# Pooled attention and top-1 experts on one core: value products in three banks handed round one by one, indices of ranked parts on VectorE, other ranks and another order

## The chip, the cores and the metric

One core of one Trainium2 chip runs the whole program in one launch. The core has TensorE (PE: matrix products, with a weight load of its own, PEld), VectorE (DVE), ScalarE (ACT), GpSimd (POOL) and SyncE (SP), each with its own queue of instructions, and 16 DMA engines. Products are summed in eight banks of PSUM; everything else lies in SBUF or in device memory. The metric is the device time of one execution in microseconds (us), the median of several runs.

## The reference

Queries are averaged in pairs, so 576 of them look at 1152 keys in each of 8 batches and 8 heads of 64 features. The 4608 rows that come out, 512 wide, go through a layer of 8 experts, of which each row takes the one with the largest gate logit.

```python
q_pool = q.reshape(B, H, S // 2, 2, D).mean(axis=3)          # B, H, S, D = 8, 8, 1152, 64
scores = scale * np.matmul(q_pool, k.transpose(0, 1, 3, 2))
scores = scores - np.max(scores, axis=-1, keepdims=True)
attn = np.exp(scores)
attn = attn / (np.sum(attn, axis=-1, keepdims=True) + 1e-09)
x = np.matmul(attn, v)                                       # -> (4608, 512)
logits = x @ w_gate                                          # w_gate (512, 8)
expert_idx = np.argmax(logits, axis=1)
gate_w = softmax(logits)[row, expert_idx]
for e in range(8):
    xe = x[expert_idx == e]
    out[expert_idx == e] = gate_w * (np.maximum(xe @ w1[e], 0.0) @ w2[e])   # w1 (512, 1024), w2 (1024, 512)
```

## The kernel before

**Attention.** The work goes by pairs of heads, and each pair by two halves of 288 queries; there are 64 such halves, eight to a batch. A half has nine score products (L543, tile `st`, two buffers of two banks each; four matmuls apiece). DVE takes each out of PSUM into the big tile `s` and keeps a running least value (L548), a small product spreads the least over the partitions (`spread`, L566), DVE makes the bias (L572), and ACT does the exponentials in three pieces (L576). POOL then adds the nine pieces of `s` up in pairs (`fold`, L622), from which PE makes the sums (L631). Nine value products (L647) go into `pa`, one tile of two banks with one buffer: ACT copies its first bank (L652), DVE adds its second bank to that (L653), and then the tile is free for the next half. With `st`, the sums and one bank for small things all eight banks are in use. Matmuls stand in a mode of small tiles there, and the profile has two records for each of them.

**Routing.** When a batch is through, logits (L722), the best expert, and a place in that expert's list are worked out (L735 to L789). Rows go to device memory (`x_runs`), and POOL scatters token numbers into `lists` (L823).

**Experts.** Two early parts of 384 rows are taken from the first seven batches; after the last batch the experts are put in order of the rows that they have left, and `RANKS` says in which parts each of them is worked: 14 ranked parts of 160 to 384 rows. A part loads its list (`li`, L908), makes an index (L918: `ix<-li,gid`; L921: four copies `rec<-li`), gathers its rows with one indirect DMA for 32 rows (L924, four of them to a tile `xr` or `xq` of 128 rows), weighs them (L1081, L1082, DVE), turns them (L1085, DVE), splits them in a high (ACT, L1089) and a low half (DVE, L1044), and multiplies: the first products (`ph`, L1138, three for each of 32 weight tiles, 96 to a part), `hh` (ACT, L1145) and `hl` (DVE, L1147), the second products (`py`, L1167, 24 for each 128 rows, 512 columns), `y` (ACT, L1185), and a scatter to the output (POOL, L1175). For the early parts SP loads the list and DVE makes the index; for the ranked parts POOL does both, in its queue with the gathers and scatters. Weights come by SP into `raw`, and ACT (L1106) and DVE (L1044) split them.

**What sets the order.** All of it is written as steps with a key, an estimated time, and the buffers they hold. A planner (`Flow`) plays the steps through: on each engine the ready step with the least key goes next, if its buffers are free by its own reckoning. A buffer comes free after the last step that holds it and an allowance (`LATE`). The sequence that comes out is fixed in the program, engine by engine. Scatters and gathers on POOL are paced: each also waits for the last PE step that the planner put ahead of it (`in_step`). Changed costs, keys and allowances therefore give another sequence.

## Time and profile before

| | us |
|---|---|
| median of three runs | 1255.66 |
| the three runs | 1249.97, 1255.66, 1256.31 |
| the profiled execution | 1251.86 |
| its span | 1250.3 |
| PE busy in the span | 1178.0 |
| POOL, DVE, ACT busy | 874.2, 769.7, 628.7 |

The span runs from the first to the last instruction; the execution has 1.56 us around it. The attention ends at about 757 us on PE, and the last scatter is issued at 1237.75 us. The granted clock of TensorE is 0.982 of full speed over the span. A busy share says how long an engine had an instruction in work, not that the work was at its best pace: a product that waits for a buffer in the middle of a run shows as a later start of the next one.

### The profile page before, as it was taken

The numbers are of one execution on the slowest core, as the hardware profiler recorded it, in microseconds if no ns is written. First come the engines' busy times: TensorE is split into PE (matmuls) and PEld (weight loads), VectorE is DVE, ScalarE is ACT, GpSimd is POOL, SyncE is SP. The second block draws the span as 40 slices with busy tenths as digits, with TensorE's granted clock in tenths as the row PEclk, the third lists the DMA queues.
The fourth block names the chain that finished last, engine by engine and source line by source line (L and its number), as shares of the span: only waits on it lengthen the run. The fifth ranks groups of instructions, "written<-read, shape, count | busy, mean of one in ns | idle before, by whom it ended". The sixth has DMA issues, their size and how long they took to land.

```text
span 1250.3 us, 33779 instructions
## 1 busy us (share of the span) xinstructions
PE 1178.0 (94%) x14157; PEld 817.4 (65%) x14157; DVE 769.7 (62%) x2080; ACT 628.7 (50%) x768; POOL 874.2 (70%) x539
## 2 busy tenths in 40 slices
PE   6999999999999999999999998968999899999995
PEld 3555555555455555555555557858888898989994
DVE  4767777767777777767767658734444453535440
ACT  3666557666566567567565446422334241423440
POOL 1999899999799799899799253576667675620110
PEclk8999999999999999999999998988999999999998
DMA  7643342353333434423424415723434352514420
GB/s 191 158 105 95 99 121 75 102 128 78 98 96 91 123 84 107 125 66 98 134 65 108 147 37 169 216 73 110 122 119 125 112 159 82 186 42 143 135 77 20
DMA packets 76082, 138.12 MB, mean 110 GB/s; under 512 B 9859, under 2 KB 33311, under 8 KB 75920
## 3 DMA queue, kind: packets, MB, share of 16 engines
q1 hardware_dynamic: 65088, 116.18, 32.6%
q0 software_dynamic: 9744, 19.64, 5.5%
q8 instruction: 114, 1.87, 0.7%
q14 instruction: 48, 0.39, 0.1%
q10 hardware_dynamic: 1088, 0.03, 0.1%
HBM read 115.04 MB, written 21.02 MB: 109 GB/s over the span
## 4 chain that ended last, share of the span: by engine, by line
PE 67%; POOL 10%; DVE 8%; issue 8%; DMA 5%; ACT 1%; POOLq 0%; SPq 0%; DVEq 0%; ACTq 0%
PE st L543 17%; PE pa L647 16%; PE py L1167 14%; PE ph L1138 12%; POOL fold L622 7%; DVE s L548 4%; PE sums L631 2%; PE st L499 2%; DMA xq<-x_runs,ix 1%; DMA xr<-x_runs,ix 1%; PE sums L617 1%; POOL lists L823 1%; DMA raw<-in_moe_w_dram 1%; PE st L505 1%; POOL out_dram L1175 1%
## 5 line engine op out<-in xcount | busy, mean ns | idle before, releaser
L548 DVE TENSOR_SCALAR_CACHE_REDUCE s<-st 128x576 f32<-128x576 f32 x576 | 419.8, 753 | 169.7 <-PE st L543 166.4
L576 ACT ACTIVATE s<-s,bias 128x1728 f32<-128x1728 f32 x192 | 322.1, 1730 | 146.4 <-DVE bias L572 142.1
L543 PE MATMUL st<-qT,kT 64*64 64x288 f32 x4608 | 362.7, 412 | 16.3 <-DVE s L548 12.6
L647 PE MATMUL pa<-s,vn 64*64 64x288 f32 x4608 | 345.6, 404 | 1.3 <-DVE xT L653 1.3
L543 PEld LDWEIGHTS st<-qT,kT 64*64 64x64 f32 x4608 | 159.4, 133 | 152.7 <-DVE s L548 65.1
L647 PEld LDWEIGHTS pa<-s,vn 64*64 64x64 f32 x4608 | 169.4, 133 | 95.7 <-DVE xT L653 6.3
L622 POOL TENSOR_TENSOR fold<-s 128x1728 f32<-128x1728 f32 x58 | 224.2, 3872 | 9.6 <-ACT s L576 9.5
L622 POOL TENSOR_TENSOR fold<-fold,s 128x1728 f32<-128x1728 f32 x58 | 224.0, 3867 | 1.0
L1138 PE MATMUL ph<-xh,w1h 128*128 128x384 f32 (+6 forms) x512 | 159.2, 311 | 17.3 <-ACT xh L1089 8.6
L924 POOL DMA_INDIRECT xr<-x_runs,ix x104 | 112.8, 1085 | 80.7 <-PE ph L1138 20.4
L1138 PE MATMUL ph<-xl,w1h 128*128 128x384 f32 (+6 forms) x512 | 157.9, 308 | 2.1 <-DVE xl L1044 2.1
L1138 PE MATMUL ph<-xh,w1l 128*128 128x384 f32 (+6 forms) x512 | 157.5, 308 | 0.0
L1175 POOL DMA_INDIRECT out_dram<-y,rec x41 | 48.6, 1185 | 137.6 <-PE py L1167 81.6
L1167 PE MATMUL py<-w2h,hl 128*128 128x512 f32 x328 | 128.9, 393 | 6.1 <-DVE hl L1147 6.1
L1167 PE MATMUL py<-w2h,hh 128*128 128x512 f32 x328 | 128.8, 393 | 0.0
L1167 PE MATMUL py<-w2l,hh 128*128 128x512 f32 x328 | 128.5, 392 | 0.0
L1147 DVE SCALAR_TENSOR_TENSOR hl<-ph,hh 128x384 fp32r<-128x384 f32 (+5 forms) x100 | 54.5, 548 | 120.0 <-ACT hh L1145 120.0
L1145 ACT ACTIVATE hh<-ph 128x384 fp32r<-128x384 f32 (+5 forms) x100 | 48.7, 487 | 151.1 <-PE ph L1138 151.1
L1138 PEld LDWEIGHTS ph<-xh,w1h 128*128 128x128 f32 x512 | 97.8, 191 | 22.2 <-DVE hl L1147 11.8
L1138 PEld LDWEIGHTS ph<-xl,w1h 128*128 128x128 f32 x512 | 97.9, 191 | 3.5 <-DVE xl L1044 2.9
L1138 PEld LDWEIGHTS ph<-xh,w1l 128*128 128x128 f32 x512 | 97.9, 191 | 0.0
L823 POOL DMA_INDIRECT lists<-re,di x48 | 45.9, 956 | 67.7 <-PE st L543 27.3
(176 smaller groups left out, 1315.6 us busy)
## 6 DMA issues: line engine op xcount, KB each, us to landing
raw<-in_moe_w_dram SPq DMA_DIRECT2D x80, 512.0 KB
qn<-in_q_dram SPq DMA_DIRECT2D x64, 384.0 KB
kn<-in_k_dram SPq DMA_DIRECT2D x32, 576.0 KB
vn<-in_v_dram SPq DMA_DIRECT2D x32, 576.0 KB
x_runs<-row SPq DMA_DIRECT2D x24, 396.0 KB
xr<-x_runs,ix POOLq DMA_INDIRECT x104, 2.7
x_runs<-empty SPq DMA_DIRECT2D x4, 297.0 KB
lists<-re,di POOLq DMA_INDIRECT x48, 6.3
```

What stands on the lines that cost most here:

```text
L543: made = nc.tensor.matmul(pt.t[to, h, :HQ], x.kT.t[up, c * P + i * D:c * P + (i + 1) * D], x.qT.t[up, cols], start=True, stop=True, tile_p ...
L548: nc.vector.tensor_scalar(s.t[:, c], pt.t[:, :, :HQ], -SCALE, None, op0=ALU.mult, op1=ALU.min, accum_out=mx.t[:, c:c + 1],)
L576: nc.scalar.activation(s.t[:, c0:c0 + n], s.t[:, c0:c0 + n], AF.Exp, bias=bias.t, scale=-1.0)
L622: add = lambda to, a, b: nc.gpsimd.tensor_tensor(to, a, b, ALU.add)
L647: made = nc.tensor.matmul(pa.t[cs, i, :HQ], x.vn.t[up, h, c, :], s.t[up, c, h], start=c == 0, stop=c == NC - 1, tile_position=(up.start, c ...
L823: ins = nc.gpsimd.indirect_dma_start(out=lists, out_offset=bass.IndirectOffsetOnAxis(ap=di.t[:, j:j + 1], axis=0), in_=re.t[:, j, :], in_o ...
L924: return nc.gpsimd.indirect_dma_start(out=x.xr[i // NQD].t[:, i % NQD, :], out_offset=None, in_=xg, in_offset=bass.IndirectOffsetOnAxis(ap ...
L1138: made = nc.tensor.matmul(view()[:, i, :], a[:, c, fp], b[:, c, :n], start=c == 0 and k == 0, stop=c == NDC - 1 and k == 2)
L1145: a = f.add("ACT", act(nb * n) - 44, lambda fs=fs, view=view: nc.scalar.activation(hidden(m)[0][:, fs, :n], view(), AF.Relu), at - 20, don ...
L1147: d = f.add("DVE", dve(nb * n), lambda fs=fs, view=view: nc.vector.scalar_tensor_tensor(hidden(m)[1][:, fs, :n], view(), 0.0, hidden(m)[0] ...
L1167: made = nc.tensor.matmul(py.t, a[:, c, hs], b[:, c % 2, :], start=c == 0 and k == 0, stop=c == NFC - 1 and k == 2)
L1175: ins = nc.gpsimd.indirect_dma_start(out=out, out_offset=bass.IndirectOffsetOnAxis(ap=x.re.t[:up, r:r + 1], axis=0), in_=y.t[:up], in_offs ...
```

## The change

- Each half's value products go into two tiles of one bank each, `pa = [bank(o), bank(o)]`, from a pool of three banks (`BANKS` 1 to 3, in place of one bank and the pair). ACT's copy frees the one, DVE's add the other.
- The index of a ranked part (L918 and L921 before, L920 and L923 after) is made by DVE instead of POOL.
- `RANKS`: the sum of rows for each rank stays; there are 13 ranked parts instead of 14, and the largest is 416 rows. Its fourth row block has 32 rows. There are 41 row blocks and 148 gathers in either program.
- Some twenty numbers of the planner: keys, costs (`spread` 130 to 185, `best` 960 to 1100, `places` 810 to 670, list loads on POOL 1400 to 1100 and later), `AHEAD` 190 to 216 (a part's gathers by key ahead of its products), `LATE` of PE 200 to 245, and 105 less for the experts' products. `K_CHAIN` is 0 and moves nothing.

```diff
-RANKS = ((384, 288), (384, 256), (384, 224), (384, 192), (384, 160), (224, 192), (352,), (160,))
+RANKS = ((384, 288), (384, 256), (352, 256), (320, 256), (288, 256), (416,), (352,), (160,))
 S_BUFS = 2
-BANKS = 5 - S_BUFS * 2
+BANKS = 7 - S_BUFS * 2
...
-K_AV = 42
+K_AV = 51
...
-AHEAD = 190
+AHEAD = 216
...
     def values(o, f, key, x, s, ready, hp, half, xT):
-        pa = hold_of("pa", lambda h: o.ps_m.tile([P, 2, 512], F32, **h.own("pa", 1)))
+        pa = [bank(o), bank(o)]
...
-                        made = nc.tensor.matmul(pa.t[cs, i, :HQ], x.vn.t[up, h, c, :], s.t[up, c, h],
+                        made = nc.tensor.matmul(pa[i].t[cs, :HQ], x.vn.t[up, h, c, :], s.t[up, c, h],
                                          start=c == 0, stop=c == NC - 1, tile_position=(up.start, cs.start))
...
-            p = f.add("PE", 452, product, key + 20.0 * c / NC, done(p, x.v, ready[c]), [pa, x.vn, s], QUADS)
-        a = f.add("ACT", act(HQ) - 44, lambda: nc.scalar.copy(xT.t[:, hp, to], pa.t[:, 0, :HQ]), key + 20, done(p), [pa, xT])
+            p = f.add("PE", 452, product, key + 20.0 * c / NC, done(p, x.v, ready[c]), [*pa, x.vn, s], QUADS)
+        a = f.add("ACT", act(HQ) - 44, lambda: nc.scalar.copy(xT.t[:, hp, to], pa[0].t[:, :HQ]), key + 20, done(p), [pa[0], xT])
         return f.add("DVE", dve(HQ), lambda: nc.vector.tensor_tensor(
-            xT.t[:, hp, to], xT.t[:, hp, to], pa.t[:, 1, :HQ], ALU.add), key + 20, done(p, a), [pa, xT])
+            xT.t[:, hp, to], xT.t[:, hp, to], pa[1].t[:, :HQ], ALU.add), key + 20, done(p, a), [pa[1], xT])
...
-            eng = nc.vector if early else nc.gpsimd
+            eng = nc.vector
...
-        p = f.carry(at, 900 if early else 1400, load, key - LEAD, [*known, *stored], [x.re, x.li], 120, 9000 * early)
-        p = f.add("DVE" if early else "POOL", 650, index, key - LEAD, done(p), [x.li, x.ix, x.re])
+        p = f.carry(at, 900 if early else 1100, load, key - LEAD, [*known, *stored], [x.re, x.li], 120, 9000 if early else 1000)
+        p = f.add("DVE", 800, index, key - LEAD, done(p), [x.li, x.ix, x.re])
...
-                    hs = slice(r * P, (r + 1) * P)
+                    hs = slice(r * P, min((r + 1) * P, TW))
+                    n = hs.stop - hs.start
...
-                            made = nc.tensor.matmul(py.t, a[:, c, hs], b[:, c % 2, :],
+                            made = nc.tensor.matmul(py.t[:n], a[:, c, hs], b[:, c % 2, :],
```

How the sequence moves shows at three places. The first is PE's queue in the third batch, where the twentieth half's value products begin. `st` rows are score products, `pa` or `m` rows value products (their number counts tiles as they are made; `m_0`, `m_1`, `m_2` are the three banks), and the L566 row is a spread. Before:

```order
L543 MATMUL st_1_3247<-qT_0_2990,kT_0_2988 64x288 x4
L543 MATMUL st_0_3252<-qT_0_2990,kT_0_2988 64x288 x4
L647 MATMUL pa_0_3166<-s_2_2815,vn_0_2495 64x288 x4
L543 MATMUL st_1_3264<-qT_0_2990,kT_0_2988 64x288 x4
L543 MATMUL st_0_3272<-qT_0_2990,kT_0_2988 64x288 x4
L543 MATMUL st_1_3278<-qT_0_2990,kT_0_2988 64x288 x4
L543 MATMUL st_0_3285<-qT_0_2990,kT_0_2988 64x288 x4
L647 MATMUL pa_0_3291<-s_3_3044,vn_0_2495 64x288 x8
L543 MATMUL st_1_3303<-qT_0_2990,kT_0_2988 64x288 x4
L566 MATMUL st_0_3310<-ident_64,top_3308 64x64 x4
```

The same place on PE after:

```order
L544 MATMUL st_0_3263<-qT_0_2961,kT_0_2959 64x288 x4
L544 MATMUL st_1_3268<-qT_0_2961,kT_0_2959 64x288 x4
L648 MATMUL m_1_3181<-s_2_2827,vn_0_2498 64x288 x2
L648 MATMUL m_2_3184<-s_2_2827,vn_0_2498 64x288 x2
L544 MATMUL st_0_3283<-qT_0_2961,kT_0_2959 64x288 x4
L544 MATMUL st_1_3288<-qT_0_2961,kT_0_2959 64x288 x4
L544 MATMUL st_0_3297<-qT_0_2961,kT_0_2959 64x288 x4
L648 MATMUL m_0_3302<-s_3_3049,vn_0_2498 64x288 x2
L648 MATMUL m_1_3305<-s_3_3049,vn_0_2498 64x288 x2
```

Between the two halves stand three score products instead of four, and the new half takes the bank that was spare and the one that ACT's copy frees. In the whole order nine runs of exactly four score products became none, runs of three went from five to three, single ones from 170 to 213; a spread is followed at once by a score product in 16 places before and in two after.

The second place is POOL's queue at the first gathers of the first ranked part (its twelve are those with `ix_10601` before and `ix_10670` after; other numbers are later parts). Before:

```order
L918 TENSOR_SCALAR ix_10651<-li_10564,gid 128x9
L921 COPY rec_3_10653<-li_10564 32x3
L921 COPY rec_3_10653<-li_10564 32x2 x3
L924 DMA xr_10670<-x_runs,ix_10601 128x132
L918 TENSOR_SCALAR ix_10685<-li_10583,gid 128x12
L921 COPY rec_4_10687<-li_10583 32x3 x4
L924 DMA xr_10670<-x_runs,ix_10601 128x132
L918 TENSOR_SCALAR ix_10711<-li_10618,gid 128x8
L921 COPY rec_5_10713<-li_10618 32x2 x4
L924 DMA xr_10670<-x_runs,ix_10601 128x132
```

POOL's queue at that place after:

```order
L910 DMA li_10691<-lists 128x1x22
L926 DMA xr_10703<-x_runs,ix_10670 128x132
L886 TENSOR_LOAD ranked
L910 ISA
L910 DMA li_10721<-lists 128x1x16
L926 DMA xr_10703<-x_runs,ix_10670 128x132 x3
L926 DMA xq_10820<-x_runs,ix_10670 128x132 x4
L926 DMA xr_10910<-x_runs,ix_10670 128x132 x4
L1178 DMA out_dram<-y_10686,rec_0_9662 4608x512
```

No index stands between the gathers any more; the list loads and scatters of output stay on POOL. The third place is DVE's queue in the second early part's first products, around its first `hl`. Before:

```order
L1044 TENSOR_TENSOR w2l_10578<-raw_10328,w2h_10577 128x1024
L1044 TENSOR_TENSOR w2l_10598<-raw_10493,w2h_10597 128x1024
L952 TENSOR_REDUCE t_rf<-t_past 1x25
L952 TENSOR_SCALAR t_sT<-sid 1x25
L952 TENSOR_TENSOR t_sT<-t_sT,t_tu 1x25
L1044 TENSOR_TENSOR w2l_10626<-raw_10506,w2h_10625 128x1024
L1147 SCALAR_TENSOR_TENSOR hl<-ph_10608,hh 128x384
```

DVE's queue at that place after:

```order
L1046 TENSOR_TENSOR w2l_10642<-raw_10439,w2h_10641 128x1024
L920 TENSOR_SCALAR ix_10670<-li_10599,gid 128x12
L923 COPY rec_2_10672<-li_10599 32x3 x4
L1046 TENSOR_TENSOR w2l_10662<-raw_10557,w2h_10661 128x1024
L1046 TENSOR_TENSOR w2l_10694<-raw_10570,w2h_10693 128x1024
L1149 SCALAR_TENSOR_TENSOR hl<-ph_10677,hh 128x384
L920 TENSOR_SCALAR ix_10732<-li_10632,gid 128x9
L923 COPY rec_3_10734<-li_10632 32x3
L923 COPY rec_3_10734<-li_10632 32x2 x3
L920 TENSOR_SCALAR ix_10749<-li_10647,gid 128x12
L923 COPY rec_4_10751<-li_10647 32x3 x4
L1149 SCALAR_TENSOR_TENSOR hl<-ph_10710,hh 128x384
```

Before, only splits of weights and pieces of the slot table (L952) stand there. After, the first index stands ahead of the last two low halves of the second weights and of the part's first `hl`, and the next two between its first two `hl`.

## Rows read from the trace of the kernel before

**Rows 1.** The page: engines' busy time, and the chain that ended last by engine.
```profile
PE 1178.0 (94%) x14157; PEld 817.4 (65%) x14157; DVE 769.7 (62%) x2080; ACT 628.7 (50%) x768; POOL 874.2 (70%) x539
...
PE 67%; POOL 10%; DVE 8%; issue 8%; DMA 5%; ACT 1%; POOLq 0%; SPq 0%; DVEq 0%; ACTq 0%
```

**Rows 2.** Stretches (the windows view): start and end, length, then busy time of PE, PEld, DVE, ACT and POOL with instructions in brackets, the granted clock, the DMA share, GB/s. Two batches of the attention, two stretches around the first ranked part, and one late stretch of the experts.
```profile
494.10:584.80 90.70, 87.37 (x1422) 50.11 (x1418) 64.78 (x196) 53.80 (x62) 85.46 (x35) 1.00 0.38 103
584.80:677.20 92.40, 88.79 (x1450) 49.67 (x1446) 67.82 (x205) 60.03 (x67) 84.60 (x35) 1.00 0.38 100
800.00:840.00 40.00, 32.36 (x149) 27.88 (x147) 14.63 (x25) 10.72 (x18) 26.65 (x47) 0.91 0.42 129
840.00:880.00 40.00, 32.78 (x157) 29.68 (x158) 17.64 (x31) 10.31 (x18) 26.25 (x33) 0.91 0.35 102
...
1100.00:1200.00 100.00, 100.00 (x619) 91.30 (x619) 45.20 (x64) 38.99 (x61) 13.29 (x12) 1.00 0.37 117
```

**Rows 3.** The chain of work that ended last, pieces in order of time: start, length, engine, line and records.
```profile
740.12 4.37 PE pa L647 x72
...
866.48 16.36 PE py L1167 x72
882.84 6.32 PE ph L1138 x48
...
945.95 11.51 PE ph L1138 x96
...
1035.66 10.70 PE ph L1138 x60
...
1062.72 10.70 PE ph L1138 x96
...
1183.43 15.46 PE ph L1138 x96
```

**Rows 4.** Timeline of POOL, 776 to 850 us.
```profile
802.48 1.25 POOL L918 TENSOR_SCALAR ix<-li,gid 128x12 int32<-128x12 int32 x1 [2.12 <-DMA li<-lists]
...
811.08 1.16 POOL L924 DMA_INDIRECT xr<-x_runs,ix  x1 [0.45 <-POOL rec L921]
...
813.94 0.62 POOL L921 COPY rec<-li 32x3 int32<-32x3 int32 x3 [0.63 <-DMA xr<-x_runs,ix]
...
817.69 0.62 POOL L921 COPY rec<-li 32x2 int32<-32x2 int32 x3 [1.24 <-DMA xr<-x_runs,ix]
...
837.46 1.00 POOL L924 DMA_INDIRECT xr<-x_runs,ix  x1 [0.30 <-issue]
838.76 1.34 POOL L924 DMA_INDIRECT xr<-x_runs,ix  x1 [0.30 <-issue]
```

**Rows 5.** Timeline of DVE, 800 to 840 us.
```profile
823.58 0.18 DVE L1081 TENSOR_TENSOR xr<-xr,li 128x16 f32<-128x16 f32 x1 [10.11 <-DMA xr<-x_runs,ix]
...
825.15 0.52 DVE L1147 SCALAR_TENSOR_TENSOR hl<-ph,hh 128x384 fp32r<-128x384 f32 x1
...
836.21 0.17 DVE L1081 TENSOR_TENSOR xq<-xq,li 128x16 f32<-128x16 f32 x1 [8.81 <-DMA xq<-x_runs,ix]
```

**Rows 6.** Timeline of PE, 814 to 847 us: the second early part's second products, and the first ranked part's first product.
```profile
814.21 0.39 PE L1167 MATMUL py<-w2h,hh 128*128 128x512 f32 x1
...
825.72 0.79 PE L1167 MATMUL py<-w2h,hl 128*128 128x512 f32 x1 [6.10 <-DVE hl L1147]
826.31 0.63 PE L1167 MATMUL py<-w2h,hh 128*128 128x512 f32 x1
826.74 0.63 PE L1167 MATMUL py<-w2l,hh 128*128 128x512 f32 x1
...
845.26 0.69 PE L1138 MATMUL ph<-xh,w1h 128*128 128x384 f32 x1 [5.95 <-ACT xh L1089]
```

**Rows 7.** Stretches again, L1138 alone: the first products of the five ranked parts of 384 rows, each from its first to its last start; columns as in rows 2 (PE, PEld).
```profile
845.26:866.32 21.06, 19.10 (x96) 18.22 (x96) 0.87 0.41 125
911.68:929.42 17.74, 16.95 (x96) 16.48 (x95) 1.00 0.49 160
968.20:988.82 20.62, 17.27 (x96) 16.47 (x95) 1.00 0.49 152
1026.81:1046.20 19.39, 16.97 (x96) 16.49 (x95) 1.00 0.47 155
1084.17:1102.07 17.90, 17.22 (x96) 16.43 (x95) 1.00 0.53 165
```

**Rows 8.** Groups of instructions (the lines view): count, busy time and mean ns of one, then idle time before them and what ended it.
```profile
L921 POOL COPY rec<-li 32x3 int32<-32x3 int32 (+2 forms) x56 | 15.5, 277 | 18.3 <-DMA xq<-x_runs,ix 6.3 <-DMA xr<-x_runs,ix 5.1 <-DMA out_dram<-y,rec 4.5
...
L918 POOL TENSOR_SCALAR ix<-li,gid 128x12 int32<-128x12 int32 (+6 forms) x14 | 7.2, 515 | 3.3 <-DMA li<-lists 2.3
...
L921 DVE COPY rec<-li 32x3 int32<-32x3 int32 x8 | 1.3, 158 | 0.1
L918 DVE TENSOR_SCALAR ix<-li,gid 128x12 int32<-128x12 int32 x2 | 0.5, 230 | 0.0
```

**Rows 9.** Timeline of all engines, 953.2 to 954 us: a split of weights on DVE and a gather on POOL.
```profile
953.30 1.23 DVE L1044 TENSOR_TENSOR w1l<-raw,w1h 128x1024 fp32r<-128x1024 f32 x1 [0.24 <-ACT w1h L1106]
...
953.41 1.98 POOL L924 DMA_INDIRECT xq<-x_runs,ix  x1 [0.42 <-PE ph L1138]
```

**Rows 10.** The tile view of `li`: from the issue of a list load to its landing.
```profile
DMA to landing us min/median/max: 2.2/3.0/5.7
```

**Rows 11.** Timeline of the third batch, 236.9 to 241 us, PE and DVE: start, length, engine, line and operation, count, and in square brackets the idle time before it and what ended it.
```profile
237.50 1.39 PE L543 MATMUL st<-qT,kT 64*64 64x288 f32 x16
...
238.97 0.75 DVE L548 TENSOR_SCALAR_CACHE_REDUCE s<-st 128x576 f32<-128x576 f32 x1
...
239.11 1.39 PE L543 MATMUL st<-qT,kT 64*64 64x288 f32 x16 [0.21 <-DVE s L548]
...
239.65 0.45 DVE L653 TENSOR_TENSOR xT<-xT,pa 128x288 f32<-128x288 f32 x1
...
240.32 0.91 PE L647 MATMUL pa<-s,vn 64*64 64x288 f32 x12
```

**Rows 12.** Timeline of PE, 411 to 416 us, around a spread.
```profile
413.63 0.34 PE L566 MATMUL st<-ident,top 64*64 64x64 f32 x8 [0.29 <-DVE s L548]
414.48 0.72 PE L543 MATMUL st<-qT,kT 64*64 64x288 f32 x8 [0.51 <-DVE bias L572]
```

More of the change, by code (lines that the diff above doesn't have):

```diff
@@ L59 @@
 DMA = 2000
-KEEP = 20
+KEEP = 21
 LAST = 3
@@ L64 @@
 WARM = 2
-SWITCH = 150
+SWITCH = 110
 CALM, CALM_X = 700, 500
-LATE = dict(PE=200, DVE=130, ACT=130, POOL=60, SP=100, DMA=1700, DMA2=1700)
+LATE = dict(PE=245, DVE=130, ACT=130, POOL=60, SP=100, DMA=1700, DMA2=1700)
 OWN = dict(PE=0, DVE=200, ACT=220, POOL=100, SP=0, DMA=0, DMA2=0)
@@ L506, in turn @@
                                             ident[up, up], tile_position=(up.start, 0))
-            s = f.add("PE", 27 * 2 * (nk + len(qs)), turn, key, after, [pt, *([kT, kp] if ks else []), *([qT, qp] if qs else [])], ROWS)
+            s = f.add("PE", 31 * 2 * (nk + len(qs)), turn, key, after, [pt, *([kT, kp] if ks else []), *([qT, qp] if qs else [])], ROWS)
             o.turned.append(s)
@@ L789, in count @@
                 nc.vector.tensor_scalar(tok, tok, float(NQ), None, op0=ALU.add)
-        p = f.add("DVE", 960, best, at + 2, done(*weighed), [*chain, pt])
-        e = f.add("ACT", 230, lambda: nc.scalar.activation(ex.t, ex.t, AF.Exp), at + 2, done(p), [ex])
-        p = f.add("DVE", 1080, first, at + 2, done(p), [pt, ohb])
-        r = f.add("PE", 360, rank, at + 3, done(p), [pr, ohb])
-        w = f.add("DVE", 640, weight, at + 3, done(p, e), [ex, re, pt])
-        p = f.add("DVE", 810, places, at + 3, done(r, w), [pr, pt, de, di])
-        c = f.add("DVE", 400, count, at + 4, done(p), [pt, lw, ex, de])
+        gap = K_CHAIN if b is not None and b < B - 2 else 0
+        p = f.add("DVE", 1100, best, at + 2 + gap, done(*weighed), [*chain, pt])
+        e = f.add("ACT", 230, lambda: nc.scalar.activation(ex.t, ex.t, AF.Exp), at + 2 + gap, done(p), [ex])
+        p = f.add("DVE", 920, first, at + 2 + 2 * gap, done(p), [pt, ohb])
+        r = f.add("PE", 360, rank, at + 3 + 2 * gap, done(p), [pr, ohb])
+        w = f.add("DVE", 640, weight, at + 3 + 3 * gap, done(p, e), [ex, re, pt])
+        p = f.add("DVE", 670, places, at + 3 + 4 * gap, done(r, w), [pr, pt, de, di])
+        c = f.add("DVE", 400, count, at + 4 + 5 * gap, done(p), [pt, lw, ex, de])
         def put(g):
```

37 lines of the change are left out of this document (19 added, 18 removed).

## The prediction

> **What bounds the kernel now.** I read the page first. PE is busy for 1178.0 of 1250.3 us and makes up 67% of the chain that ended last; POOL and DVE follow with 10% and 8% [rows 1]. So the kernel goes at the pace of PE, and what can be won is PE work taken out, or places where PE stands or creeps. The windows show where these are. In a steady batch PE is busy for 87.37 of 90.70 us, and POOL, the next, for 85.46 [rows 2]: little is idle there, though a run of products that waits for buffers can count as busy in part. Around the first ranked part PE is busy for only 32.36 and 32.78 us of 40, and the granted clock falls to 0.91, while from 1100 to 1200 it is never idle [rows 2]. The timeline of those stretches then names the wait, and the chain gives the price of products at full pace.
>
> **Parts of the experts (term A).** A part's first products are 96 matmuls whatever its width. The chain prices 96 of them at 10.70 us for 192 columns, 11.51 for 256, 12.64 for 288 (48 in 6.32), 15.46 for 352, and 17.1 for 384 (60 in 10.70) [rows 3]. I take 10.7 for 160 and 224 as well, since the group's products of 192 columns are at what looks like a floor, 14.05 for 320 (halfway from 288 to 352), and 18.6 for 416 (1.5 past 384, by the slopes on either side, 1.4 to 1.6 for 32 columns). Before: 5 x 17.1 + 12.64 + 11.51 + 6 x 10.7 + 15.46 = 189.3. After: 2 x 17.1 + 2 x 12.64 + 4 x 11.51 + 2 x 15.46 + 14.05 + 18.6 + 10.7 = 179.8. The second products are priced by row blocks, 24 matmuls of 512 columns or 5.45 us each (72 in 16.36 [rows 3]), and both programs have 41. **A = -9.5**, between -9.2 and -9.8.
>
> **Start of the ranked parts (term B).** Here POOL decides. The first list lands, the index is made at 802.48, the first gather goes at 811.08 and the twelfth at 838.76: 28 us for twelve gathers that follow one another every 1.30 us when nothing stands between them [rows 4]. Between them stand the indices of later parts, whose copies `rec` each time wait for the gather just issued to land (at 813.94 and 817.69 [rows 4]). DVE stands for 10.11 us before it can weigh the first tile, with an `hl` queued behind; PE lacks that `hl` for 6.10 us in the middle of the second early part, and once it goes on, its products start 0.43 us apart (826.31 to 826.74) where they take 0.227 at full pace [rows 3, 5, 6]. A second wait of 8.81 us on DVE for the next tile leaves PE idle for another 5.95 [rows 5, 6]. So the second products of that part took from 814.21 to 845.26, 31.05 us for 16.36 of work, and the next first products 21.06 for 17.1 [rows 3, 6, 7]: 14.7 + 4.0 = 18.7 us lost.
>
> After the change the index is off POOL, and the queue there shows twelve gathers with one list load among them, each paced by a product of the second early part. What is new is that DVE's first index waits for the list, with two splits of second weights and the first `hl` behind it; those in turn hold back ACT and PE. An index costs DVE 0.23 + 4 x 0.158 = 0.86 us [rows 8], a split 1.23 [rows 9]. Before, POOL had the list at 802.48 [rows 4]; if DVE has it then too, the first `hl` comes after it by one index and two splits, 3.3 us, and I put the end of the first products 4.3 us later for it: **B = 4.3 - 18.7 = -14.4**. Bounds: -18.7 if the list is there before DVE comes to it, since the last `lists` scatter stands earlier in PE's order; -10 if it takes 5.7 us to land in place of the median of 3.0 [rows 10] and two more indices fall in ahead of that `hl` (4.4 us more).
>
> **Later gathers (term C).** The other four parts of 384 rows took 17.74, 20.62, 19.39 and 17.90 us, 75.65 in sum where 4 x 17.1 = 68.4 is their work [rows 7]: 7.2 us of waiting for gathered rows in the middle of the first products. POOL lost 7.2 + 15.5 us in indices and 3.3 + 18.3 in waiting for them [rows 8], 44.3 over 14 parts, and it made the gathers late by as much. Without these, and with gathers that stand earlier by key (`AHEAD` 190 to 216), they should lie a whole second product ahead: **C = -7**, between 0 and -7.2. DVE takes 13 x 0.86 = 11 us in exchange, beside a PE that is busy all the while: from 1100 to 1200 DVE has 45.20 of 100 us in work [rows 2]. The cover is gone only where the index itself has to wait for its list, which takes 2.2 to 5.7 us from issue to landing [rows 10].
>
> **Attention (term D).** A value product takes 0.485 us in a run (72 records in 4.37 [rows 3]). Where four score products stand in a row, PE goes at the pace at which DVE takes them: from 237.50 to 240.32 are 2.82 us for four, 0.88 more than 4 x 0.485 [rows 11]. They stand in a row because the next half's value products need the tile that DVE adds at 239.65 [rows 11]. After the change such runs are gone (nine to none): -7.9. A spread that a score product follows costs a wait for the bias, 0.51 us in the row shown [rows 12]; 16 such places become two. Some of these have other work that is late anyway, so I take -6 for 14 of them. Against this the new order has a third more single score products, 43 of them, which would cost 2 us at 0.05 each; that is an estimate without a row, since single ones in the trace of before don't stand out. **D = -12**, between -18 and 0; a loss is not excluded, as the keys move folds and sums too: in the new order a half's sums stand somewhat nearer to its scores, so that POOL, busy for 85.46 of 90.70 us [rows 2], has less time to fold. Ahead of the first batch and behind the last scatter I see nothing that changes.
>
> **Sum.** -9.5 - 14.4 - 7 - 12 = -42.9. From the profiled execution's 1251.86 us that gives 1209. The profiled execution is 3.8 us under the median of the three runs, 1255.66; I don't add that, since the three spread over 6.3 us. About 0.5%, 6.3 us, is what a measurement of this kernel can tell from no change.
>
> **Rivals.** *Attention gives nothing.* POOL's folds would become the last of a half. For: POOL has only 5 us of air in a batch [rows 2], and sums that stand earlier find it late. Against: the air is over three times what D asks of a batch, 1.5 us. Price: D is gone, 1251.86 - 31 = 1221.
>
> *The gathers stay late.* They are paced by products, and each needs some 2.8 us to land (the copies after the gather at 811.08 go on at 813.94 [rows 4]); if that and not the index set the pace, B and C are gone and A and D stay: 1230. Against it speak gathers every 1.30 us where no index lies between, paced in the same way.
>
> *DVE's index stops POOL.* The gather at 953.41 took 1.98 us beside a split of weights on DVE, against 1.00 alone [rows 4, 9]. If each index stopped POOL for its own length, 13 x 0.86 = 11 us would come back at worst: 1220; at the start alone, six indices, 5 us: 1214. The Trainium skill (SBUF — State Buffer, "Who interferes with whom") says that a copy or a tensor_scalar of DVE can hold the port pair that it shares with GpSimd for the whole instruction, and that the other then blocks fully. The longer gather agrees with such a rule as far as it goes, though the split is an instruction with two inputs in SBUF, which the page lists apart.
>
> *All of the waits are only moved.* Both of the first two: A alone is left, 1242.
>
> *Slower: DVE waits for lists.* Each index stands in DVE's queue ahead of `hl` and of the splits. If each found its list just issued, DVE would stand for up to 5.7 us [rows 10], 13 times, and PE behind it: 74 us, so 1283. It decides, that is, eats up the gain, from 43 / 13 = 3.3 us for each. Against it: in the new order only the first few indices stand close to their list's load; for later ones enough products stand between that, at 0.178 to 0.227 us each [rows 3], they make 4 us or more.
>
> *The change doesn't do what it says.* The names of the banks in the new order show the pairs going round, and no index on POOL, so only the size is open.
>
> **How the numbers follow.** Forecast (1209): 0.50. Attention gives nothing (1221): 0.22. Gathers late (1230): 0.14. DVE stops POOL (1214 to 1220): 0.06. Both first rivals (1242): 0.05. DVE waits for lists: 0.03. The forecast's own bounds are 1251.86 - 9.8 - 18.7 - 7.2 - 18 = 1198 and, with B at -10 and C at half, 1217. The range 1195 to 1234 leaves out the last two cases, 0.08, and the tails of the others, some 0.1. Faster by over 0.5% than the median, so under 1249.4: 0.94, all but the slower case and 0.03 of the case at 1242, whose neighbours reach that far. Within 0.5%: 0.03. Slower: 0.03.
>
> **What would show it.** Right: a batch of 90.5 to 91 us; no run of four score products, and no wait of a value product for L654's add; twelve gathers of the first ranked part within 17 us; no PE idle time over 2 us between the second early part and the end; the four parts of 256 columns at 11.5 us each. Wrong on B: PE idle in the second early part with DVE waiting for `li` or for `xr`. Wrong on C: an idle DVE before `xq` or `xr` with PE behind it. Wrong on D: batches of 92 us with waits for folds or for DVE's takes. Wrong on the whole: waits of DVE's index for `li` of several us in every part.

## The result, and the profile after

| | before | after |
|---|---|---|
| median, us | 1253.33 (4 runs) | 1223.37 (4 runs, 1221.79 to 1224.7) |
| profiled execution, us | 1251.86 | 1222.86 |
| its span, us | 1250.3 | 1221.3 |

The ratio is 0.9761, with a 95% interval from 0.9728 to 0.9794: 30 us faster. The forecast was 1209, so 14 us of the 43 are missing, and the time lies close to the first rival's 1221, though not for that rival's reason. The page of the changed kernel, its busy times and its chain by engine:

```profile
PE 1169.4 (96%) x14061; PEld 826.4 (68%) x14061; DVE 781.7 (64%) x2145; ACT 629.7 (52%) x768; POOL 854.4 (70%) x468
...
PE 78%; POOL 6%; DVE 5%; issue 4%; DMA 4%; ACT 2%; POOLq 0%; SPq 0%; DVEq 0%
```

PE's share of the chain went from 67 to 78% [rows 1]. Two batches, and the stretch from the second early part's first product to the end of the first ranked part's first products (windows view of the changed kernel, columns as in rows 2):

```profile
446.88:535.92 89.04, 87.64 (x1436) 53.88 (x1432) 66.58 (x200) 57.03 (x63) 85.21 (x35) 1.00 0.41 104
535.92:625.30 89.38, 87.97 (x1436) 53.71 (x1432) 66.58 (x200) 57.12 (x63) 85.20 (x35) 1.00 0.40 104
779.95:840.02 60.07, 52.53 (x265) 48.70 (x264) 36.19 (x87) 21.12 (x32) 34.62 (x32) 0.94 0.55 167
```

Batches take 89.0 to 89.4 us instead of 90.7 to 92.4 [rows 2], with POOL at 85.2 as before: it did not become the bound. The whole attention, from the start of its first score product to the start of its last value product, went from 737.5 (13.67 to 751.15) to 722.1 us (12.52 to 734.58). Where four score products stood in a row [rows 11], PE's timeline of the changed kernel has this:

```profile
234.24 1.39 PE L544 MATMUL st<-qT,kT 64*64 64x288 f32 x16
235.84 0.72 PE L544 MATMUL st<-qT,kT 64*64 64x288 f32 x8 [0.21 <-DVE s L549]
236.38 0.67 PE L648 MATMUL m<-s,vn 64*64 64x288 f32 x8
```

and DVE's timeline this:

```profile
236.38 0.45 DVE L654 TENSOR_TENSOR xT<-xT,m 128x288 f32<-128x288 f32 x1
```

The new half begins while the add that it used to wait for is only starting. The part around the first ranked part took 60.07 us instead of 69.92 (796.40 to 866.32 in the trace of before), 9.85 less where 14.4 were forecast. Its DVE and POOL rows:

```profile
786.84 0.23 DVE L920 TENSOR_SCALAR ix<-li,gid 128x12 int32<-128x12 int32 x1 [6.70 <-DMA li<-lists]
786.98 0.67 DVE L923 COPY rec<-li 32x3 int32<-32x3 int32 x4
787.69 2.36 DVE L1046 TENSOR_TENSOR w2l<-raw,w2h 128x1024 fp32r<-128x1024 f32 x2
789.96 0.55 DVE L1149 SCALAR_TENSOR_TENSOR hl<-ph,hh 128x384 fp32r<-128x384 f32 x1
...
791.27 0.23 DVE L920 TENSOR_SCALAR ix<-li,gid 128x12 int32<-128x12 int32 x1
791.41 0.85 DVE L923 COPY rec<-li 32x3 int32<-32x3 int32 x4
```

```profile
780.10 0.78 POOL L910 DMA_DIRECT2D li<-lists  x1 [6.03 <-DMA lists<-re,di]
...
787.90 1.96 POOL L926 DMA_INDIRECT xr<-x_runs,ix  x1 [2.07 <-DVE rec L923]
...
790.88 1.07 POOL L926 DMA_INDIRECT xr<-x_runs,ix  x1 [0.30 <-issue]
...
810.86 1.26 POOL L926 DMA_INDIRECT xr<-x_runs,ix  x1 [0.37 <-PE py L1170]
```

and PE's row behind them (its timeline, then the windows view of all engines, columns as in rows 2):

```profile
790.57 0.69 PE L1140 MATMUL ph<-xh,w1h 128*128 128x384 f32 x1 [6.22 <-DVE hl L1149]
...
790.57:793.00 2.43, 2.43 (x8) 2.43 (x9) 2.30 (x13) 0.00 (x0) 1.07 (x2) 0.50 0.88 298
```

DVE stands 6.70 us for the list, the two splits and the `hl` come behind it as the order said, and PE waits 6.22; the products right behind that wait go at a granted clock of 0.50, the lower level of 1.2 GHz. After that the second products run without a break (16.7 us instead of 31.05), and the first ranked part begins without a wait: its twelve gathers, from 787.90 to 810.86, are in time. Of the ranked parts, the first gained (18.46 us instead of 21.06 [rows 7]), but PE waits in it and in three later ones (first products alone, windows view, columns as in rows 7; widths 384, 352, 320 and 288):

```profile
821.56:840.02 18.46, 17.13 (x96) 16.66 (x95) 1.00 0.48 156
942.52:960.41 17.89, 15.86 (x96) 15.15 (x95) 1.00 0.55 167
999.67:1021.68 22.01, 16.96 (x96) 16.51 (x95) 0.84 0.40 125
1060.93:1074.72 13.79, 13.31 (x96) 12.76 (x95) 1.00 0.64 201
```

The part of 320 rows takes 22.01 us for some 14.3 of work, and the granted clock falls to 0.84 in it. Two rows of the chain say why, and that one more thing had changed:

```profile
903.43 16.70 PE py L1170 x72
...
1001.53 7.22 DMA xr<-x_runs,ix
```

The timelines of DVE and PE show the wait, and the windows view what follows it:

```profile
1008.88 0.18 DVE L1083 TENSOR_TENSOR xr<-xr,li 128x16 f32<-128x16 f32 x1 [5.78 <-DMA xr<-x_runs,ix]
1009.70 0.88 DVE L1149 SCALAR_TENSOR_TENSOR hl<-ph,hh 128x320 fp32r<-128x320 f32 x2
...
1010.24 0.63 PE L1140 MATMUL ph<-xh,w1h 128*128 128x320 f32 x1 [5.05 <-DVE hl L1149]
...
1010.24:1013.00 2.76, 2.76 (x10) 2.76 (x11) 0.34 (x1) 0.00 (x0) 0.00 (x0) 0.50 0.00 0
```

A gather takes 7.22 us from issue to landing; DVE stands 5.78 for it with two `hl` queued behind, PE waits 5.05 for the first of them, and then goes at a granted clock of 0.50 (1.2 GHz) for a while. Counted through, this gather is the 115th of the 148 and belongs to the third part further on, whose first product comes at 1091. The wait in the first ranked part is of the same kind: DVE weighs rows of the next part at 829.34, after 2.21 us for their gather, and PE lacks the `hl` behind it for 1.32. So were the waits of this stage before the change; DVE and PE in the part that began at 1026.81 [rows 7], in the trace of before:

```profile
1034.24 0.17 DVE L1081 TENSOR_TENSOR xr<-xr,li 128x16 f32<-128x16 f32 x1 [3.92 <-DMA xr<-x_runs,ix]
1035.06 1.01 DVE L1147 SCALAR_TENSOR_TENSOR hl<-ph,hh 128x384 fp32r<-128x384 f32 x2
...
1035.66 0.44 PE L1138 MATMUL ph<-xh,w1h 128*128 128x384 f32 x1 [2.42 <-DVE hl L1147]
```

And 72 second products take 16.70 us where they took 16.36 [rows 3].

### The profile page after: what moved, and what is told of

It reads as the page before. It is cut to its first block, busy times and chain, and to the rows that moved or that the text cites. A ratio compares the mean times of both kernels' runs of the same rounds, so it can differ in the third digit from the quotient of the medians.

```text
span 1221.3 us, 33596 instructions
## 1 busy us (share of the span) xinstructions
PE 1169.4 (96%) x14061; PEld 826.4 (68%) x14061; DVE 781.7 (64%) x2145; ACT 629.7 (52%) x768; POOL 854.4 (70%) x468
## 4 chain that ended last, share of the span: by engine, by line
PE 78%; POOL 6%; DVE 5%; issue 4%; DMA 4%; ACT 2%; POOLq 0%; SPq 0%; DVEq 0%
PE st L544 19%; PE m L648 18%; PE py L1170 17%; PE ph L1140 15%; POOL fold L623 5%; PE sums L632 3%; DVE s L549 2%; PE st L500 2%; PE sums L618 1%; POOL lists L825 1%; ACT s L577 1%; DMA xr<-x_runs,ix 1%; PE st L506 1%; DMA lists<-re,di 1%; DMA xq<-x_runs,ix 1%
## 5 line engine op out<-in xcount | busy, mean ns | idle before, releaser
L544 PE MATMUL st<-qT,kT 64*64 64x288 f32 x4608 | 372.3, 410 | 9.9 <-DVE s L549 6.7
L648 PE MATMUL m<-s,vn 64*64 64x288 f32 x4608 | 363.2, 405 | 0.0
L544 PEld LDWEIGHTS st<-qT,kT 64*64 64x64 f32 x4608 | 169.5, 133 | 140.0 <-DVE s L549 57.0
L648 PEld LDWEIGHTS m<-s,vn 64*64 64x64 f32 x4608 | 182.1, 133 | 84.6 <-ACT xT L653 2.6
L1140 PE MATMUL ph<-xh,w1h 128*128 128x384 f32 (+6 forms) x480 | 152.5, 318 | 17.8 <-DVE hl L1149 15.0
L1140 PE MATMUL ph<-xl,w1h 128*128 128x384 f32 (+6 forms) x480 | 151.0, 315 | 0.5 <-DVE xl L1046 0.5
L1140 PE MATMUL ph<-xh,w1l 128*128 128x384 f32 (+6 forms) x480 | 150.5, 313 | 0.0
L1170 PE MATMUL py<-w2h,hh 128*128 128x512 f32 (+1 forms) x328 | 129.6, 395 | 0.0
L1170 PE MATMUL py<-w2h,hl 128*128 128x512 f32 (+1 forms) x328 | 129.3, 394 | 0.0
L1170 PE MATMUL py<-w2l,hh 128*128 128x512 f32 (+1 forms) x328 | 128.9, 393 | 0.0
L1140 PEld LDWEIGHTS ph<-xh,w1h 128*128 128x128 f32 x480 | 92.4, 193 | 22.0 <-DVE hl L1149 17.2
L1188 ACT COPY y<-py 128x512 f32<-128x512 f32 (+3 forms) x41 | 24.0, 586 | 124.0 <-PE py L1170 114.7
```

Source lines behind the costliest of these rows:

```text
L544: made = nc.tensor.matmul(pt.t[to, h, :HQ], x.kT.t[up, c * P + i * D:c * P + (i + 1) * D], x.qT.t[up, cols], start=True, stop=True, tile_p ...
L648: made = nc.tensor.matmul(pa[i].t[cs, :HQ], x.vn.t[up, h, c, :], s.t[up, c, h], start=c == 0, stop=c == NC - 1, tile_position=(up.start, c ...
L1140: made = nc.tensor.matmul(view()[:, i, :], a[:, c, fp], b[:, c, :n], start=c == 0 and k == 0, stop=c == NDC - 1 and k == 2)
L1170: made = nc.tensor.matmul(py.t[:n], a[:, c, hs], b[:, c % 2, :], start=c == 0 and k == 0, stop=c == NFC - 1 and k == 2)
```

## The experiments

Kernels were timed in three groups, each on a chip of its own beside the kernel before. The chips differ (before: 1253.8, 1265.4 and 1257.2 us), so times are compared as ratios, and stages by the trace. "Attention" is as above; "rest" runs from the start of the last value product to the end of the last second product. On the second chip the four kernels have an attention of 728 to 730 us where the same runs of products took 722 to 724 on the others, so there the rest is read; no trace of the kernel before was kept on that chip, so what of the rest is the chip's own is not known. b_tw416 and b_ixdve have the attention of before in the same order, on two chips, at 739.4 and 739.0 us against 737.5: a difference of 2 us there says nothing.

| kernel | median, us | ratio to before | 95% | attention | rest |
|---|---|---|---|---|---|
| before (first profile) | 1253.33 | | | 737.5 | 485.7 |
| changed | 1223.37 | 0.9761 | 0.9728 to 0.9794 | 722.1 | 473.7 |
| b_banks | 1243.59 | 0.9931 | 0.9909 to 0.9952 | 731.6 | 483.6 |
| a_pair | 1255.25 | 0.9999 | 0.9974 to 1.0024 | 746.1 | 482.5 |
| b_tw416 | 1260.22 | 1.0051 | 1.0028 to 1.0073 | 739.4 | 495.3 |
| a_ranks | 1217.4 | 0.9716 | 0.9673 to 0.9758 | 721.9 | 471.2 |
| a_ixpool | 1242.83 | 0.9834 | 0.9807 to 0.9861 | 727.6 | 487.3 |
| a_g3000 | 1218.38 | 0.9637 | 0.9611 to 0.9664 | 728.2 | 463.4 |
| a_l6000 | 1225.73 | 0.9702 | 0.9673 to 0.973 | 728.5 | 469.5 |
| m_parts384 | 1230.54 | 0.9731 | 0.9701 to 0.9761 | 730.0 | 474.6 |
| b_ixdve | 1241.14 | 0.987 | 0.9827 to 0.9913 | 739.0 | 474.3 |
| m_gl | 1209.69 | 0.9619 | 0.9577 to 0.966 | 722.4 | 459.3 |
| a_kav42 | 1240.53 | 0.9854 | 0.9808 to 0.99 | 728.9 | 484.3 |
| a_h448 | 1219.15 | 0.9685 | 0.9639 to 0.9731 | 723.8 | 469.3 |

**b_banks: the three banks alone, in the kernel before.**

```diff
-BANKS = 5 - S_BUFS * 2
+BANKS = 7 - S_BUFS * 2
...
-        pa = hold_of("pa", lambda h: o.ps_m.tile([P, 2, 512], F32, **h.own("pa", 1)))
+        pa = [bank(o), bank(o)]
```

> The kernel before with the value products' halves in three banks, and nothing else of the change. In its order, runs of four score products between value products fall from 12 (with the start-up) to 1, and a spread is followed by a score product in 5 places instead of 16. Theory (the banks bring the attention's gain): the first product of the experts starts some 10 to 13 us earlier than the 757.4 us of before, the experts' stage keeps its length, and the time is about 1241. Rival (the keys and the new order bring it, the banks alone nothing): within 4 us of before, about 1250.

The time is 10 us less, but only 5.9 of it in the attention, and most batches still take 88 to 92 us. All but one of the runs of four did go, as the order said; runs of three (11 instead of 5) and of five and more (4 instead of 1, without the 12 at the start) came in their place. All runs of three and more, the 12 at the start aside, lasted 14.4 us longer in the trace than 0.485 us a product, where they had cost 12.7 before and cost 4.8 in the changed kernel. Neither theory holds as it stood.

**a_pair: the pair of banks again, in the changed kernel** (the diff above the other way round, with the changed keys).

> The changed kernel with the value products in one tile of two banks again (one spare bank, keys and the rest as changed). In its order there are 11 runs of four score products and 6 spreads followed by a score product. Theory (banks): the experts start 8 to 12 us later than the 740.8 us of the changed kernel, and the time is about 1232 to 1235. Rival (keys): at most 3 us later, under 1227.

All of the gain is gone: the attention takes 746.1 us, 24 more than the changed kernel's, twice what the theory asked, and 8.6 more than before the change. So the changed keys and costs alone are worse than nothing, the banks alone bring 5.9, and both together 15.4. The steady batches have the same order: from the first score product of the fourth batch to that of the eighth, a batch takes 91.4 us before, 92.4 in a_pair, 90.0 in b_banks and 89.1 in the changed kernel.

**a_kav42: one key back.**

```diff
-K_AV = 51
+K_AV = 42
```

> The changed kernel with the key of value products at its old 42 instead of 51. In its order there are 13 runs of three to six score products instead of 6. Theory (the banks give the freedom, the key puts the value products where they break up the runs of score products): 4 to 8 us more than the changed kernel, ratio to before 0.979 to 0.983. Rival (the banks and any key do): ratio 0.976 to 0.978.

The attention is 6.8 us longer than the changed kernel's, as expected in size, but the ratio misses the theory's range (0.985 for 0.979 to 0.983), and the theory's reason is not shown. Runs of three and more do come back, at 11.2 us instead of 4.8, but a steady batch takes 89.2 us, as with the key at 51 (89.1). The loss is in the second batch (2.6 us) and behind the first score product of the last (3.8). In the trace its last product ends 18 us later than the changed kernel's, which was not expected: the last batch's routing is no longer filled with the early part's products. From its last value product to the first product of the experts 17.8 us pass instead of 6.3, at a granted clock of 0.65 (742.25 to 760.05, windows view).

```profile
742.25:760.05 17.80, 5.48 (x47) 3.19 (x39) 15.18 (x33) 13.06 (x27) 14.29 (x12) 0.65 0.60 188
```

**b_tw416: only the distance between rows, in the kernel before.**

```diff
-    TW = max(n for ns in RANKS for n in ns)
+    TW = 416
```

> The kernel before with room for 416 columns in the tiles of tokens and hidden values (so rows of 1664 bytes instead of 1536), parts and all else as before. Theory (the distance between rows sets the rate): three row blocks of second products take 16.70 us instead of 16.36, over 41 row blocks 4.6 us more, first products of 256 and 352 columns some 1 per cent less; in sum 2 to 4 us more than before. Rival (the partial row block, or something else in the changed kernel, makes the second products slower): 16.36 stays and so does the time.

The chain has this for second products; the partial row block and the other parts are not in this kernel:

```profile
872.64 16.70 PE py L1167 x72
```

The theory holds for the rate. The time is 6 us longer instead of 2 to 4; in the trace, which is of the slowest of ten executions, the first products of three parts of 384 rows, the second early one among them, take 1.0 to 3.2 us longer too.

**a_h448: rows of 1792 bytes for the hidden values, in the changed kernel.**

```diff
-            m.h = tuple(m.w.tile([P, NFC, TW], F32R, name=a) for a in ("hh", "hl"))
+            m.h = tuple(m.w.tile([P, NFC, 448], F32R, name=a) for a in ("hh", "hl"))
```

> The changed kernel with rows of 1792 bytes (room for 448 columns) in the hidden values, 1664 in the tokens. Theory one (products whose weights come from rows that aren't a multiple of 512 bytes apart are slower): second products stay at 16.70 us for three row blocks. Theory two (a multiple of 256 bytes does): 16.36 again, 4.6 us less.

Theory two: the chain has the old rate again, and the rest is 4.4 us shorter.

```profile
906.26 16.34 PE py L1170 x72
```

**a_ranks: the parts of before, in the changed kernel.**

```diff
-RANKS = ((384, 288), (384, 256), (352, 256), (320, 256), (288, 256), (416,), (352,), (160,))
+RANKS = ((384, 288), (384, 256), (384, 224), (384, 192), (384, 160), (224, 192), (352,), (160,))
```

> The changed kernel with the parts of before (16 first products of parts instead of 15, 384 columns at most, so rows of 1536 bytes). Theory (distance between rows): second products at 16.36 us for three row blocks again, 4.6 us less in sum, against 9.5 us more for the first products by the prediction's term A: about 1228. Rival (second products at 16.70 whatever the parts): about 1233.

Both theories expected it to be slower than the changed kernel, by 5 us and by 10. It is not: 0.9716 against 0.9761, with intervals that overlap. Second products are at 16.36 for 72 and 4.6 us less in sum; first products, with one part more, take only 2.0 us more (238.2 against 236.2, the stretches from first to last start added), because the waits are smaller: 6.2 us in the later parts of 384 rows where the changed kernel has 11.2 in its three of 352, 320 and 288. In the two traces the new parts by themselves are a loss of some 2.5 us in the rest.

**m_parts384: the changed parts without the one of 416.**

```diff
-RANKS = ((384, 288), (384, 256), (352, 256), (320, 256), (288, 256), (416,), (352,), (160,))
+RANKS = ((384, 288), (384, 256), (352, 256), (320, 256), (288, 256), (224, 192), (352,), (160,))
```

> The changed kernel with its parts except for the last but two: 224 and 192 rows in place of one part of 416, so that no part is over 384 rows and rows are 1536 bytes apart. Theory (term A holds for the parts and the distance between rows costs 4.7 us): against the changed kernel second products 4.6 us less, first products 3.3 us more by 10.7 + 10.7 - 18.1, 0.8 less in the four parts of 384: 2 us less, and 5 us less than the same kernel with the parts of before, 1217.4, so 1212 to 1221. Rival (narrower first parts of an expert bring gathers and weights of the next closer together, and PE waits there): no faster than with the parts of before, 1217 or more.

The rival: 0.9731, no faster than a_ranks. Second products are at 16.36, yet the parts of 352, 320 and 288 rows take 18.83, 21.85 and 15.00 us, 13 more than without waits (15.46, 14.16 and 13.05 in m_gl below).

**a_ixpool: the index on POOL again, in the changed kernel.**

```diff
-            eng = nc.vector
+            eng = nc.vector if early else nc.gpsimd
...
-        p = f.add("DVE", 800, index, key - LEAD, done(p), [x.li, x.ix, x.re])
+        p = f.add("DVE" if early else "POOL", 800, index, key - LEAD, done(p), [x.li, x.ix, x.re])
```

> The changed kernel with the index of ranked parts on POOL again. Theory (POOL's index makes the first gathers late, as in the prediction's term B): from the first to the twelfth gather of the first ranked part 24 to 28 us instead of 23, DVE waits for rows with hl behind, PE idle 5 us or more in the second early part's second products; 6 to 10 us more, 1230 to 1233. Rival (the landing of lists and gathers sets the pace, not the engine of the index): within 3 us of 1223.

The theory, and by the trace more than its 6 to 10 us: the rest is 13.5 us longer (by the ratios it is some 9). The first ranked part's twelve gathers take 28.7 us from the first to the last issue instead of 23.0. PE's timeline has the two gaps of before [rows 6] again, somewhat wider:

```profile
817.10 0.79 PE L1170 MATMUL py<-w2h,hl 128*128 128x512 f32 x1 [8.87 <-DVE hl L1149]
...
836.84 0.69 PE L1140 MATMUL ph<-xh,w1h 128*128 128x384 f32 x1 [6.80 <-ACT xh L1091]
```

and POOL's timeline has its copies that wait for gathers:

```profile
801.79 1.13 POOL L926 DMA_INDIRECT xr<-x_runs,ix  x1 [0.28 <-POOL rec L923]
...
805.32 0.63 POOL L923 COPY rec<-li 32x3 int32<-32x3 int32 x3 [1.85 <-DMA xr<-x_runs,ix]
```

**b_ixdve: the index on DVE alone, in the kernel before** (the same lines the other way).

> The kernel before with the index of ranked parts on DVE and nothing else of the change. Theory (the index on POOL makes the first gathers late): the second early part's second products take 16.4 us instead of 31, its first products 20 to 25 instead of 17.8, since DVE stands for the first list with hl behind it; 7 to 10 us less than before, a ratio of 0.992 to 0.995. Rival (only together with the other order does it help): ratio 0.998 or more.

More than expected: a ratio of 0.987, 16 us; in the trace the rest is 11.4 us shorter. The second products of the second early part take 16.36 us, its first products 28.34, with DVE at the index for 8.99 us:

```profile
805.05 0.23 DVE L918 TENSOR_SCALAR ix<-li,gid 128x12 int32<-128x12 int32 x1 [8.99 <-DMA li<-lists]
```

The later waits fell too: parts of 384 rows at 17.61, 16.67, 18.98 and 17.23 us, 3.8 over four times 16.67, where before they were 9.0 over. One thing did not come as the prediction had it: with no index between them the twelve gathers still take 28.6 us from first to last, as before (27.7). What moved is the first of them, from 14.7 to 8.4 us after the second early part's first product.

**a_g3000: gathers are given 3 us more to land.**

```diff
-... [x.ix, x.xr[i // NQD]], 400, paced=CALM if early else CALM_X)
+... [x.ix, x.xr[i // NQD]], 400, 0 if early else 3000, paced=CALM if early else CALM_X)
```

> The changed kernel in which the planner allows 3 us more for a ranked part's gathers to land, so that the weighing of gathered rows stands later in DVE's queue, behind more of the hl. The attention's order is the same. Theory (PE's waits in the later parts, 2.1, 5.4 and 0.7 us, come from DVE standing at a weighing for rows that land in 5 to 7 us beside loads of weights, with hl behind it): these waits go, 6 to 8 us less, about 1216. Rival (the gathers are issued too late for their part, wherever DVE waits for them): the waits move to the first products of the next part, within 2 us of 1223.

In time the theory, and more than it asked: the rest is 10.3 us shorter. The same parts of 384, 352, 320 and 288 rows as in the windows of the changed kernel:

```profile
828.37:846.53 18.16, 17.18 (x96) 16.78 (x96) 1.00 0.48 156
949.04:964.40 15.36, 15.36 (x96) 15.23 (x95) 1.00 0.60 179
1003.71:1018.00 14.29, 14.29 (x96) 13.92 (x95) 1.00 0.61 204
1057.20:1070.40 13.20, 13.10 (x96) 12.74 (x95) 1.00 0.70 224
```

PE no longer waits in the last three. But the reason is not the one expected. Of 41 weighings, 33 stand behind exactly as many `hl` as in the changed kernel; of the four in front of its longest waits (829.34, 953.15, 1008.88 and 1070.10), three do, and the fourth stands behind one fewer. The row at 1008.88 of the changed kernel, on DVE here:

```profile
1006.61 0.48 DVE L1149 SCALAR_TENSOR_TENSOR hl<-ph,hh 128x320 fp32r<-128x320 f32 x1
1007.01 0.16 DVE L1083 TENSOR_TENSOR xr<-xr,li 128x16 f32<-128x16 f32 x1
...
1007.84 0.49 DVE L1149 SCALAR_TENSOR_TENSOR hl<-ph,hh 128x320 fp32r<-128x320 f32 x1
```

It has the same place, behind the part's first `hl`, and no wait. What moved is the gather: it was issued 1.9 us after the first product of the part of 320 rows (1001.53 against 999.67), and the same one, by its place among the 148, goes 3.5 us ahead of that product here (1000.2 against 1003.7). The last gathers of those four tiles go 10, 26, 27 and 31 products earlier in PE's order. So the run shows that an earlier gather takes the waits away; a later weighing was not tried.

**a_l6000: lists are given 5 us more to land.**

```diff
-..., load, key - LEAD, [*known, *stored], [x.re, x.li], 120, 9000 if early else 1000)
+..., load, key - LEAD, [*known, *stored], [x.re, x.li], 120, 9000 if early else 6000)
```

> The changed kernel in which the planner allows 5 us more for a ranked part's list to land, so that the first index stands behind both last splits of weights and three more hl of the second early part. Theory (DVE stands 6.7 us at the first index for the list, with the splits and the hl behind it): the second early part's first products take 18 to 19 us instead of 24.9; 4 to 6 us less, about 1218. Rival (the gathers come later by as much as DVE is freed): PE waits for the first ranked part's rows instead, within 2 us of 1223.

The rest is 4.2 us shorter, at the lower end of the theory. Here the waiting step did move back: the first index stands behind both splits and two `hl` (three had been expected), and DVE's waits for lists fall from 10.9 to 1.2 us.

```profile
790.92 0.56 DVE L1149 SCALAR_TENSOR_TENSOR hl<-ph,hh 128x384 fp32r<-128x384 f32 x1 [0.48 <-ACT hh L1147]
791.89 0.23 DVE L920 TENSOR_SCALAR ix<-li,gid 128x12 int32<-128x12 int32 x1 [0.41 <-DMA li<-lists]
```

The early part's first products fall from 24.90 to 18.99 us, but its second products and the next first products give back 2.35 and 1.34 (19.06 and 19.80), where the rows now come later: part of the rival.

**m_gl: these together.** The parts of m_parts384 with both allowances.

> The changed kernel with no part over 384 rows (224 and 192 in place of 416), 3 us more allowed for gathers to land and 5 us more for lists. Theory (the three causes add up: distance between rows, DVE's standing for gathers, DVE's standing for the first list): the experts' stage takes 452 to 455 us where the changed kernel took 467.5, ratio to before about 0.960. Rival (the waits of the parts with 352 to 384 rows come back, as they did with these parts and the old allowances): stage 462 or more, ratio 0.966 or more.

The rest is 459.3 us, and from the first product of the experts to the last 453.0, as the theory has it; the ratio is 0.9619, 1209.69 us, the fastest kernel here, though a_g3000 (0.9637) lies within its interval. The parts of before with both allowances were not tried, so the new parts are not shown to help here either. Behind the second early part's start PE waits for more than 1 us only once, and the four narrower parts run clean:

```profile
819.41 0.44 PE L1140 MATMUL ph<-xh,w1h 128*128 128x384 f32 x1 [4.31 <-ACT xh L1091]
```

## Why the prediction was right, and where it was wrong

The range held the time and the sign was right. Of the terms, in the profiled execution's own numbers: -29.0 us in all, of them -16.6 up to the last value product, +0.1 to the second early part, -9.85 there, -2.2 from there to the end of the last product, and -0.5 in the tail. That the time still fell into the range is in part luck: from the last value product on, -12.4 came where A, B and C had -30.9, and ahead of it more than D had, most of it by things that D had not named. Of the signs named beforehand, batches came out better (89.0 to 89.4 us for 90.5 to 91), and two failed: the twelve gathers took 23.0 us where 17 was the bound, and PE stood over 2 us twice, for 6.22 and 5.05.

**A, the parts.** The mechanism was right; the size in clean products is -8.4 (170.5 before and 162.1 after for the parts behind the first ranked one, taken from parts in which PE doesn't wait). The price of 17.1 for 384 columns came from 60 products that weren't all at full pace; 96 without a wait take 16.67. What failed is the step "both programs have 41" row blocks at 5.45 us each: the wider tiles, which I had not priced, made each row block 0.113 us dearer, +4.0 over the 35 row blocks behind that point. b_tw416 and a_h448 show that it is the distance between rows. In sum the new parts brought nothing, as a_ranks shows: the dearer row blocks took back half, and the waits of the narrower parts the rest.

**B, the start of the ranked parts.** That the index on POOL cost the stall in the second early part was right, shown both ways by b_ixdve and a_ixpool; that indices spread the twelve gathers holds in the new order (a_ixpool: 28.7 us against 23.0) and not in the old (b_ixdve: 28.6 against 27.7). The step "I put the end of the first products 4.3 us later" was too small: 7.1 (24.90 against 17.81). The list was there 6.89 us after the part's start and not, as before, 6.08, and the splits took 2.36 us behind it, as reckoned. The rest is the clock, which the step left out: 24.90 us less 16.87 of work and 6.22 of waiting leaves 1.8, for products at 0.50 of the clock behind the wait. The first ranked part's own products gained 2.6 instead of 4.0, for PE waits 1.32 us in it for an `hl` behind a weighing of the next part's rows.

**C, the later gathers.** This failed. The step "it made the gathers late by as much" put all of the 7 us down to POOL's indices. Measured against 16.67, four parts lost 9.0 us before, and after the change three parts lose 11.2, with POOL free of the index. b_ixdve shows that in the old order the index was worth 5.2 of the 9.0. In both orders PE waits for `hl`, behind a weighing at which DVE stands for a gather. The new order has its gathers too late for the place that it gives their weighings, and `AHEAD` at 216 did not mend that; a_g3000, with the gathers earlier and the weighings where they were, takes the waits away. I had written that an idle DVE before `xr` with PE behind it would show C wrong, and that is the row at 1008.88.

**D, the attention.** -15.4, and 1.2 more ahead of it, where -12 stood, inside the bounds. The step "such runs are gone: -7.9" measures -6.4 in the trace (9 runs of four, 7.7 us over 0.485 a product; one new run of five after, 1.3). The spreads gave 4.4 (16.0 to 11.6 us in all). The finer alternation cost 4.8 where I put 2: single value products with a score product behind went from 136 to 213 and their excess from 4.7 to 9.5 us. So the steps that I named come to -6.0, half of D, and that D was near is luck; the remaining 9.4 us are in work that I had not counted and that no run takes apart. And the reason given was only half of one: b_banks frees the banks and brings 5.9 us, a_pair gives the keys without the banks and loses 8.6. The bank is what allows another order; the keys are the order. What each of the other keys does was not tried.

**Rivals.** POOL did not become the bound of the attention (85.2 us busy of 89). The gathers did stay late in the later parts, as the second rival had it, but not in the first ranked one, and what made them late is their place in the order, which a_g3000 moves. DVE's index doesn't stop POOL: the gather at 790.88 took 1.07 us beside two indices, while the one at 787.90 took 1.96 beside splits of weights. By the page that I named (the Trainium skill, SBUF — State Buffer, "Who interferes with whom") an instruction of DVE with two inputs in SBUF contends with one of GpSimd that reads SBUF: the split is such a one, and the trace agrees with that part of it. The slower rival's mechanism, a DVE that waits for lists, is there twice (10.9 us in two waits for `li`), at the start, and nowhere later.

## What to carry to other kernels

Here DVE took its work in the order of its queue, so a step that stood for a transfer held up all that was queued behind it. There are two cures: issue the transfer earlier (a_g3000: 3 us more for a landing in the planner's reckoning, and no faster transfer, were worth 10 us), or put the step that waits further back (a_l6000: worth 4). When such a plan is changed, look in the trace which of the two moved. A buffer that comes free earlier is worth only what the order makes of it: time both halves of such a change alone before adding them up. And when a change widens a tile, look at the rate of products that it doesn't mention.

## What the runs showed of the hardware

- Second products (24 for a row block, 512 columns each) whose stationary operand, the hidden values, lies in rows of 1664 bytes take 16.70 us for 72 (the changed kernel, b_tw416), in rows of 1536 or 1792 bytes 16.36 and 16.34 (before, a_h448). First products that read their columns from rows of 1664 bytes are slower at 384 columns (16.87 against 16.67 for 96) and faster at 256 and 352 (11.41 against 11.51, 15.25 against 15.46).
- A gather's issue takes 1.01 us beside nothing on DVE (28 gathers of the changed kernel after 760 us) or beside an index alone (4). Where a split of weights was already running as it began, it takes 1.73 in the mean, up to 2.04 (23); where a split began during it, 1.06 (6).
- A gather's landing takes 2.75 us from its issue in the mean where no load of expert weights was issued in the 12 us before it (25 gathers of the changed kernel after 760 us), and 3.86 where one or more were (37), at most 6.77; the one at 1001.53, whose landing the chain alone gives, took 7.22. That the loads are the cause was not tried by a run.
- Behind waits of 6.22 and 5.05 us PE went on at a granted clock of 0.50 (1.2 GHz), as the windows from 790.57 and 1010.24 show.
